# Five attention units by hand before block 0, weight decoding in quarters, and block 0 alone for sixteen slots

## The chip, the cores and the metric

The kernel runs on one core of one Trainium2 chip. The metric is the device time of one execution in microseconds; lower is better.

## The reference

The input is a linear attention with a decaying state over 4 batches, 8 heads, 768 steps and head dimension 48. Its output, 3072 tokens of 384 values, goes through two feed-forward layers with 2048 hidden values each. Everything is float32.

```python
for t in range(S):                                   # S = 768
    cur = einsum('bhd,bhe->bhde', u * k[t], v[t])
    y[t] = einsum('bhd,bhde->bhe', r[t], state + cur)
    state = w[..., None] * state + einsum('bhd,bhe->bhde', k[t], v[t])
x = y as (3072, 384)
h = x @ w_in1;  x = max(0.01 * h, h) @ w_out1        # layer 0
h = x @ w_in2;  x = (h * cos(h)) @ w_out2            # layer 1
```

## The kernel before

**Attention** is cut into 24 units of 128 tokens, six for each batch, and each unit into two chunks of 64. Units 0 to 7 (`u < ONE`) are built by `early(u)`, which returns the steps of a unit by name: `X R Z` (VectorE: the keys, queries and a third tensor times powers of the decay), `PK` and `NK` (32 matmuls, then a ScalarE copy), `PA` and `PD` (32 matmuls of scores each), `M N` (two VectorE selects out of PSUM), `PU S1 PV S0` (the new state; a "lean" unit does the state's sums on VectorE, the others fold them into matmuls and copy on ScalarE). `piece_y1` makes the output of the unit, which GpSimd's DMA queue writes to `xt` in DRAM (line 493), reads back as `xl` (`load_xu`, line 563), and `split_xu` splits into a high and a low part (a ScalarE cast at line 567, a VectorE subtraction at 568). Units 8 to 23 run through `prep`, `piece_a` and `piece_y` with fewer steps.

**The feed-forward layers** run over 12 blocks of 512 tokens (6 in each layer) times 16 weight chunks. One such pair is a slot. `g1` has nine matmuls of 128x128 by 128x512 (line 580), `evac_a` and `evac_b` evacuate it (for layer 0: ScalarE line 589, VectorE 590, ScalarE 607, VectorE 608), and two slots later (`LAG`) `g2` has nine matmuls into three accumulators (lines 620 to 622). So 192 slots have 3456 large matmuls.

**Weights** come packed, 768 KB for a chunk (`load_w`, line 140), and `split_w` decodes one with three ScalarE instructions (lines 281, 285, 286) and five of VectorE (282, 283, 290, 291, 294).

**Order.** SyncE's DMA queue runs in program order. For ScalarE, VectorE and TensorE the list `first` writes the order by hand for units 0 to 3 with four whole decodes; all after it is ordered by a planner that simulates the timeline. Block 0 is alone for `LB` = 8 slots, and the rest of block 0 alternates with block 1. Units 5 to 7 lie in the first slots of block 0, each chunk is decoded just before its first slot, and weight chunks 13 to 15 are loaded after the output of unit 7, since their buffers are lent to attention (the three states `ss_`, the keys `nk_`, one output). Units from 8 on are put into the slots by `due`; block 2 needs units 8 to 11.

Of the kernel before, what the change touches and what calls it, by code (L numbers as in the profile page):

```python
# [21 lines left out]
HC = C // 2  # L22
# [14 lines left out]
LB = 8  # L37
GB = 2
LATE = 8
HOLD = 16  # L40
# [3 lines left out]
FIRST = 3  # L44
# [13 lines left out]
def moe_rwkv_kernel(ctx: ExitStack, tc, wT, uT, wq, uu, rs, ks, nat, wmoe, out):  # L58
# [36 lines left out]
    ss_ = [halves(lent(*i)) for i in ((15, 0), (15, 1), (14, 0))]  # L95
    nk_ = halves(lent(14, 1))
    nk_ = [nk_[:, i] for i in range(2)]
# [53 lines left out]
    for f in range(4):  # L151
        load_w(0, f)
# [28 lines left out]
    for i in range(4):  # L181
        nc.gpsimd.memset(vf_[i][64:128, 0], 0.0)
        nc.gpsimd.memset(vf_[i][0:64, 1], 0.0)
        if i < 3:
            nc.gpsimd.memset(ss_[i], 0.0)
    sm = ap_.tile([D, H, D], F32, name="sm")
    ub = ap_.tile([128, H, D], F32, name="ub")

    def decays():
        nc.vector.tensor_scalar(out=ws, in0=wt, scalar1=W_LO, scalar2=W_HI, op0=ALU.max, op1=ALU.min)  # L190
        for i in range(H):
# [7 lines left out]
        nc.gpsimd.tensor_tensor(out=wd, in0=wc, in1=wc, op=ALU.mult)  # L199
# [9 lines left out]
    def in_range():  # L209
        ge = const.tile([PACK, H], F32, name="ge")  # L210
        cnt = const.tile([PACK, 1], F32, name="cnt")
        flag = const.tile([1, 1], I32, name="flag")
        nc.vector.tensor_tensor(out=ge, in0=ws, in1=wt, op=ALU.is_equal)
        nc.vector.tensor_reduce(out=cnt, in_=ge, axis=AX.X, op=ALU.min)
        tot = psum.tile([1, 1], F32, tag="a1", name="tot")
        nc.tensor.matmul(out=tot, lhsT=cnt, rhs=ones, start=True, stop=True)
        nc.vector.tensor_scalar(out=flag, in0=tot, scalar1=PACK - 0.5, scalar2=None, op0=ALU.is_lt)
        return nc.values_load(flag[0:1, 0:1], min_val=0, max_val=1)
# [55 lines left out]
    def split_w(L, f):  # L274
# [11 lines left out]
        nc.scalar.copy(out=mid[:, :, :, 0], in_=part[:, :, :, 1])  # L286
# [10 lines left out]

# [4 lines left out]
    def early(u):  # L302
        x, r, z, ar, vs = kf_[ring(u)], rf_[ring(u)], zf_[u % 2], ar_[u % 2], v_of(u)
        n, st = nk_[u % 2], ss_[u % 3]
        s0, s1 = st[HALF[1], 0], st[HALF[0], 1]
        nxt = (ss_[(u + 1) % 3] if u + 1 < ONE else vs_[1 - u % 2])[HALF[1], 0]
        last = u % NCH == NCH - 1
        first, lean = u % NCH == 0, u >= UB
# [38 lines left out]
        def PU():  # L347
            o = bank_of("pu")
            fold = not first and not lean
            if fold:  # L350
                nc.tensor.matmul(out=o[HALF[1]], lhsT=ident[0:PACK, HALF[1]], rhs=st[0:PACK, 0], start=True, stop=False)
# [39 lines left out]
    E = {}  # L391
# [29 lines left out]
    def piece_a(u):  # L421
        if u < ONE:
            return step("PK NK PA PD PU S1 PV S0 M N", u)
# [52 lines left out]
    def piece_y1(u):  # L476
        ar = ar_[u % 2]
        vs, ss = (t.rearrange("t c h d -> t (c h d)") for t in (v_of(u), ss_[u % 3]))
        py = psum.tile([PACK, H, HC], F32, tag=f"{bank(u)}2", name="py")
        for g in range(H):  # L480
# [4 lines left out]
            for c in range(1 if u % NCH == 0 else 0, 2):  # L485
                nc.tensor.matmul(
                    out=py[HALF[c], g], lhsT=ss[0:PACK, cols(H * c + g, D)], rhs=rf_[ring(u)][:, g],
                    start=False, stop=True)
        yo = yo1 if u % 2 else ap_.tile([PACK, H, HC], F32, tag="yo", bufs=YOB, name="yo")
# [22 lines left out]
    def do_piece():  # L512
# [8 lines left out]
        else:  # L521
            piece_y(i)
            if i == ONE - 1:
                for f in range(13, NF):
                    load_w(0, f)
            if i + 2 >= 6:
                fetch(i + 2)
# [57 lines left out]
    def evac_a(slot):  # L585
        p = hp.pop(slot)
        ga = mp.tile([128, NB], F32, tag="ga", bufs=2, name="ga")
        if blocks[slot[0]][0] == 0:
            nc.scalar.activation(out=ga, in_=p, func=AF.Copy, scale=0.01)  # L589
            nc.vector.tensor_tensor(out=ga, in0=p, in1=ga, op=ALU.max)  # L590
        else:
            gt = mp.tile([128, NB], F32, tag="gt", bufs=2, name="gt")
            nc.scalar.activation(out=ga, in_=p, func=AF.Copy, scale=INV2PI, bias=0.25)  # L593
            nc.scalar.activation(out=gt, in_=ga, func=AF.Copy, bias=MAGIC)  # L594
            nc.vector.scalar_tensor_tensor(  # L595
                out=gt, in0=gt, scalar=MAGIC, in1=ga, op0=ALU.subtract, op1=ALU.subtract)
            nc.vector.tensor_scalar(  # L597
                out=gt, in0=gt, scalar1=0.5, scalar2=-0.5, op0=ALU.min, op1=ALU.max)
            nc.scalar.activation(out=gt, in_=gt, func=AF.Sin, scale=-TWOPI)  # L599
            nc.vector.tensor_tensor(out=ga, in0=p, in1=gt, op=ALU.mult)  # L600
        ev[slot] = ga
# [46 lines left out]
    for j in range(1, N1):  # L648
        a = 0 if j == 1 else at[0][1] + LAG + 1 if j == 2 else at[2][0] + PACE * (j - 3)
        b = a + PACE if j > 2 else at[j][0] - (2 if j == 1 else 4)  # L650
        n = ends[j] - ends[j - 1]
        for q in range(FIRST if j == 1 else 0, n):
            due.setdefault(a + (b - a) * q // n, []).append(q)

    def decode():
        split_w(0, ready[0])
# [6 lines left out]
    def decode2():  # L663
# [4 lines left out]
        split_w(1, ready2[0])  # L668
# [14 lines left out]
    with tc.manual_schedule(engines={mybir.EngineType.Activation, mybir.EngineType.DVE, mybir.EngineType.PE}):  # L683
        decays()
        for k, u in first:
            if k == "if":
                slow = in_range()
                step_by_step()
                rest_of_loads()
            elif k not in do:  # L690
                step(k, u)
            else:
                do[k](u)
                if k == "y":
                    load_xu(u)
    for f in range(10, 13):
        load_w(0, f)
    kn = ap_.tile([128, H, D], F32, name="kn")
    ps = psum.tile([128, H, D], F32, tag="a1", name="ps_t")
    for c, g, a, b in flip(pt[:, 1]):  # L700
        nc.tensor.matmul(out=ps[TOK[c], g], lhsT=a, rhs=b, start=True, stop=True)
    nc.scalar.copy(out=kn, in_=ps)
    npc[0] = ends[0]
    while npc[0] < ends[0] + FIRST:
        do_piece()
    split_xu(UB - 1)

    for si in range(len(slots) + LAG):
        if si < len(slots):
            slot = j, f = slots[si]  # L710
            while j == 0 and ready[0] < min(f + AHEAD, NF):
                decode()
            g1(slot)
            evac_a(slot)
        if 1 <= si <= len(slots):
            evac_b(slots[si - 1])
        if si < len(slots):
            for _ in due.get(si, ()):
                do_piece()
            if npc[0] >= len(pieces) and not rest:  # L720
# [55 lines left out]
```

## Time and profile before

| | |
|---|---|
| median of three runs | 965.49 us (964.47 to 969.25) |
| the profiled execution | 967.88 us |
| its span, from the first to the last instruction | 966.3 us |
| TensorE busy | 918.0 us, 95% of the span |
| VectorE busy | 634.6 us, 66% |
| ScalarE busy | 543.9 us, 56% |

The 1.58 us between the profiled execution and its span lie outside the instructions. Busy TensorE is not TensorE at its peak: its matmuls overlap, and small ones count as busy too.

### The profile page before, as it was taken

The page shows a single profiled execution, that of the slowest core. Times are in us where ns is not written, and L with a number is a line of the kernel's source. Part 1 is how long each engine was busy: PE and PEld are TensorE (multiplying, and loading weights), DVE is VectorE, ACT ScalarE, POOL GpSimd, SP SyncE. Part 2 cuts the span into 40 slices and gives each one's busy share as a digit, 9 for nine tenths or more (in the row PEclk, how much of TensorE's full clock was granted, in tenths as well). Part 3 has the DMA queues.
Part 4 walks back from the last instruction along what each step waited for, and adds up shares of the span by engine and source line. Part 5 has one row for each costly group of instructions (what it writes and reads, how often), then busy time and mean ns, then how long its engine had stood idle before and what let it go on. Part 6 is the DMA issues. An engine that isn't in the chain of part 4 may idle for free.

```text
span 966.3 us, 16453 instructions
## 1 busy us (share of the span) xinstructions
PE 918.0 (95%) x6536; PEld 759.3 (79%) x6536; DVE 634.6 (66%) x1042; ACT 543.9 (56%) x1043; POOL 53.2 (6%) x93
## 2 busy tenths in 40 slices
PE   5747998999999999999999999999999999999997
PEld 4746786888777888888788888888888888888886
DVE  6379938338875667574776986666656655665654
ACT  2456536434664555453746786665665655665654
POOL 3111110000100000000000000000000000000000
PEclk9867999999999999999999999999999999999999
DMA  7931143004431242231514520010100100100000
GB/s 241 303 114 55 43 139 78 1 22 127 148 117 51 84 122 65 61 115 48 199 33 164 164 98 34 21 46 1 33 34 1 51 16 1 65 1 1 34 1 33
DMA packets 31552, 71.55 MB, mean 74 GB/s; under 512 B 4464, under 2 KB 7664, under 8 KB 31472
## 3 DMA queue, kind: packets, MB, share of 16 engines
q1 hardware_dynamic: 21824, 47.66, 15.8%
q0 software_dynamic: 4896, 14.16, 4.8%
q10 hardware_dynamic: 4752, 8.65, 2.4%
q8 instruction: 51, 0.84, 0.4%
q14 instruction: 29, 0.24, 0.1%
HBM read 56.30 MB, written 14.16 MB: 73 GB/s over the span
## 4 chain that ended last, share of the span: by engine, by line
PE 79%; DVE 7%; DMA 6%; ACT 2%; issue 2%; SPq 0%; POOL 0%; DVEq 0%; ACTq 0%; POOLq 0%
PE ph L580 37%; PE po L620 13%; PE po L621 12%; PE po L622 12%; DMA raw<-in_wmoe 3%; PE py L465 1%; PE pa L429 1%; DMA kst<-in_ks 1%; PE pu L436 1%; DMA xt<-lent 1%; DVE w L290 1%; DVE gl L608 1%; DVE ar L405 1%; DVE ar L442 1%; DMA ar<-in_rs 1%
## 5 line engine op out<-in xcount | busy, mean ns | idle before, releaser
L580 PE MATMUL ph<-xh,w 128*128 128x512 f32 x1152 | 301.6, 390 | 0.0
L580 PEld LDWEIGHTS ph<-xh,w 128*128 128x128 f32 x1152 | 217.2, 189 | 45.6
L620 PE MATMUL po<-gh,w 128*128 128x512 f32 x576 | 227.6, 395 | 4.3 <-ACT gh L607 4.1
L621 PE MATMUL po<-gh,w 128*128 128x512 f32 x576 | 224.6, 390 | 0.0
L622 PE MATMUL po<-gl,w 128*128 128x512 f32 x576 | 208.1, 390 | 0.0
L608 DVE TENSOR_TENSOR gl<-ga,gh 128x512 fp32r<-128x512 f32 x192 | 132.3, 689 | 115.1 <-ACT gh L607 102.7
L607 ACT CAST gh<-ga 128x512 fp32r<-128x512 f32 x192 | 118.8, 619 | 134.2 <-PE po L621 91.6
L580 PE MATMUL ph<-xl,w 128*128 128x512 f32 x576 | 167.5, 394 | 3.1 <-DVE ga L590 3.1
L620 PEld LDWEIGHTS po<-gh,w 128*128 128x128 f32 x576 | 108.1, 188 | 28.9 <-ACT gh L607 5.7
L580 PEld LDWEIGHTS ph<-xl,w 128*128 128x128 f32 x576 | 108.1, 189 | 26.5 <-DVE ga L590 4.0
L622 PEld LDWEIGHTS po<-gl,w 128*128 128x128 f32 x576 | 107.9, 188 | 22.6
L621 PEld LDWEIGHTS po<-gh,w 128*128 128x128 f32 x576 | 108.2, 188 | 21.5
L590 DVE TENSOR_TENSOR ga<-ph,ga 128x512 f32<-128x512 f32 x96 | 66.0, 689 | 47.8 <-ACT ga L589 47.3
L589 ACT ACTIVATE ga<-ph 128x512 f32<-128x512 f32 x96 | 56.9, 594 | 64.6 <-PE ph L580 63.0
L595 DVE SCALAR_TENSOR_TENSOR gt<-gt,ga 128x512 f32<-128x512 f32 x96 | 65.9, 690 | 38.7 <-ACT gt L594 38.3
L600 DVE TENSOR_TENSOR ga<-ph,gt 128x512 f32<-128x512 f32 x96 | 65.8, 688 | 34.3 <-ACT gt L599 33.6
L599 ACT ACTIVATE gt<-gt 128x512 f32<-128x512 f32 x96 | 59.9, 627 | 49.2 <-DVE gt L597 48.9
L593 ACT ACTIVATE ga<-ph 128x512 f32<-128x512 f32 x96 | 57.4, 597 | 42.5 <-PE ph L580 29.2
L441 ACT ACTIVATE ar<-ident,bon 64x64 f32<-64x64 f32 x256 | 64.5, 333 | 17.0 <-DVE bon L408 16.7
L594 ACT ACTIVATE gt<-ga 128x512 f32<-128x512 f32 x96 | 60.3, 631 | 2.1 <-ACT ga L593 0.4
L597 DVE TENSOR_SCALAR gt<-gt 128x512 f32<-128x512 f32 x96 | 40.4, 424 | 1.9
L281 ACT ACTIVATE ds<-raw 128x768 f32<-128x768 f32 x32 | 29.1, 913 | 17.0 <-DMA raw<-in_wmoe 12.6
(134 smaller groups left out, 787.4 us busy)
## 6 DMA issues: line engine op xcount, KB each, us to landing
raw<-in_wmoe SPq DMA_DIRECT2D x32, 768.0 KB, 7.2
natt<-in_nat SPq DMA_DIRECT2D x16, 384.0 KB, 3.7
kst<-in_ks SPq DMA_DIRECT2D x22, 224.0 KB, 3.2
x2t<-ob ACTq DMA_DIRECT2D x18, 256.0 KB, 2.0
xl<-x2t POOLq DMA_DIRECT2D x6, 768.0 KB, 4.8
vs<-in_nat SPq DMA_DIRECT2D x44, 96.0 KB, 3.7
xt<-yo POOLq DMA_DIRECT2D x40, 96.0 KB, 3.3
out<-ob ACTq DMA_DIRECT2D x15, 256.0 KB, 2.0
```

The source lines that it names most:

```text
L441: nc.scalar.activation(out=ar[q, c, g], in_=ident2[q], func=AF.Copy, scale=bon[q, g:g + 1])
L580: nc.tensor.matmul(out=p, lhsT=w_[:, 0, k * 128:(k + 1) * 128], rhs=x_[:, k], start=(m == 0), stop=(m == 3 * KT - 1))
L590: nc.vector.tensor_tensor(out=ga, in0=p, in1=ga, op=ALU.max)
L594: nc.scalar.activation(out=gt, in_=ga, func=AF.Copy, bias=MAGIC)
L595: nc.vector.scalar_tensor_tensor(out=gt, in0=gt, scalar=MAGIC, in1=ga, op0=ALU.subtract, op1=ALU.subtract)
L599: nc.scalar.activation(out=gt, in_=gt, func=AF.Sin, scale=-TWOPI)
L600: nc.vector.tensor_tensor(out=ga, in0=p, in1=gt, op=ALU.mult)
L607: nc.scalar.copy(out=gh, in_=ga)
L608: nc.vector.tensor_tensor(out=gl, in0=ga, in1=gh.bitcast(F32), op=ALU.subtract)
L620: nc.tensor.matmul(out=o, lhsT=w_l[:, 1, sl], rhs=gh, start=(f == 0), stop=False)
L621: nc.tensor.matmul(out=o, lhsT=w_h[:, 1, sl], rhs=gh, start=False, stop=False)
L622: nc.tensor.matmul(out=o, lhsT=w_h[:, 1, sl], rhs=gl, start=False, stop=(f == NF - 1))
```

## The change

Five units (`SOLO`) instead of four are ordered by hand ahead of block 0. Their states live in two pairs of tiles that share the buffers of `gt` and `ob`, which the layers use later, and `nk_` in `kn` and `ub`, whose own contents are made after unit 7 (`late_tables`). The lent weight buffers 14 and 15 are thereby free, weight chunks 8 to 15 are loaded after unit 4, and loads of units 8 and 9 are held until the first prep piece. `split_w` becomes a generator of four parts, and a `quarter` of it stands between the steps. The order by hand now reaches through the first 16 slots (`HAND`), which are all of block 0's; units 5 to 7 are spread over slots 0 to 12, with four quarters of decoding in each slot until the weights are done. The second half of a unit's step, `PU S1 PV S0`, waits in the list `after` until the slot's `g2`. The range test (`flag`) is computed at the start instead of after unit 0's scores, `wd` moves from GpSimd to VectorE, and six matmuls of zeros (`stir`) run at the start.

```diff
-LB = 8
+LB = 16
-HOLD = 16
+HOLD = 99
-FIRST = 3
+SOLO = 5
+HAND = 16
...
-    ss_ = [halves(lent(*i)) for i in ((15, 0), (15, 1), (14, 0))]
-    nk_ = halves(lent(14, 1))
+    ss_ = [[mp.tile([128, NB], F32, tag=n, bufs=2, name=n)[:, 0:DM].rearrange("p (h d) -> p h d", h=H)
+            for n in ("gt", "ob")] for i in range(2)]
+    nk_ = [kn, ub]
...
+    def stir(n):
+        o = psum.tile([128, DM], F32, tag="h", bufs=2, name="stir")
+        for i in range(n):
+            nc.tensor.matmul(out=o, lhsT=still[:, 0:128], rhs=still, start=i == 0, stop=i == n - 1)
...
     def decays():
...
+        nc.vector.tensor_tensor(out=ge, in0=ws, in1=wt, op=ALU.is_equal)
+        nc.vector.tensor_reduce(out=cnt, in_=ge, axis=AX.X, op=ALU.min)
+        stir(3)
+        nc.tensor.matmul(out=tot, lhsT=cnt, rhs=ones, start=True, stop=True)
+        stir(3)
...
+        nc.vector.tensor_scalar(out=flag, in0=tot, scalar1=PACK - 0.5, scalar2=None, op0=ALU.is_lt)
...
-        nc.gpsimd.tensor_tensor(out=wd, in0=wc, in1=wc, op=ALU.mult)
+        nc.vector.tensor_tensor(out=wd, in0=wc, in1=wc, op=ALU.mult)
...
     def split_w(L, f):
...
+        nc.scalar.copy(out=mid[:, :, :, 0], in_=part[:, :, :, 1])
+        yield
         nc.scalar.activation(out=s, in_=top.bitcast(F32), func=AF.Sign)
+        yield
...
         nc.scalar.activation(out=a, in_=a, func=AF.Relu, scale=8.0, bias=rebias)
-        nc.scalar.copy(out=mid[:, :, :, 0], in_=part[:, :, :, 1])
+        yield
...
-        first, lean = u % NCH == 0, u >= UB
+        first, lean = u % NCH == 0, u >= SOLO
...
-            return step("PK NK PA PD PU S1 PV S0 M N", u)
+            return step("PK NK PA PD M N", u) or after.append(("PU S1 PV S0", u))
...
+    first = [("R Z", 0), ("X R Z", 1), ("if", 0), ("PK NK PA PD M N", 0), ("d", 0)]
+    for u in range(SOLO - 1):
+        first += [("PK NK", u + 1), ("d", 0), ("PU S1", u), ("d", 0), ("PA", u + 1), ("PV S0", u),
+                  ("PD", u + 1)]
+        first += [("X R Z", u + 2)] if u + 2 < SOLO else [("x", 0)]
+        first += [("d", 0), ("d", 0), ("y", u)]
+        first += {0: [("l", 4), ("w", 5)], 1: [("l", 5), ("w", 6), ("w", 7)]}.get(u, [])
+        first += [("M N", u + 1)]
+    u = SOLO - 1
+    first += [("PU S1 PV S0", u), ("x", 1), ("x", 2), ("y", u), ("l", 6)] + [("w", f) for f in range(8, NF)]
+    first += 3 * [("d", 0)] + [("x", 3), ("X R Z", SOLO), ("d", 0), ("d", 0)]
...
     for si in range(len(slots) + LAG):
+        if si == HAND:
+            hand.close()
         if si < len(slots):
             slot = j, f = slots[si]
-            while j == 0 and ready[0] < min(f + AHEAD, NF):
-                decode()
             g1(slot)
+        if si < HAND:
+            e0, e1 = evac_0(slot), evac_2(slot)
+            next(e0)
+            quarter()
+            next(e0)
+            next(e1)
+            quarter()
+            next(e1)
+        elif si < len(slots):
             evac_a(slot)
...
             for _ in due.get(si, ()):
                 do_piece()
+            if si < HAND:
+                quarter()
+                quarter()
+            if npc[0] >= ends[1] and not late_split:
+                late_split.append(1)
+                split_xu(2 * UB - 1)
...
             g2(slots[si - LAG])
+            while after:
+                step(*after.pop(0))
```

## Rows read from the trace of the kernel before

**Rows 1.** Stretches: PE, PEld, DVE, ACT, POOL busy us; granted clock, DMA share, GB/s.
```profile
0.00:20.00 20.00, 8.57 (x139) 8.13 (x140) 12.84 (x30) 4.86 (x13) 8.80 (x27) 1.00 0.83 261
20.00:40.00 20.00, 19.66 (x457) 17.78 (x456) 8.79 (x14) 9.90 (x15) 2.42 (x3) 1.00 0.82 275
40.00:80.00 40.00, 22.71 (x399) 20.84 (x399) 25.86 (x41) 19.67 (x28) 7.01 (x9) 0.66 0.46 141
80.00:120.00 40.00, 33.24 (x457) 28.13 (x457) 38.86 (x63) 23.60 (x34) 4.76 (x6) 0.91 0.18 48
120.00:160.00 40.00, 35.11 (x341) 29.08 (x338) 24.95 (x41) 17.17 (x26) 4.06 (x6) 0.96 0.44 131
160.00:966.30 806.30, 798.75 (x4755) 655.35 (x4753) 523.35 (x857) 468.75 (x929) 26.20 (x42) 1.00 0.19 60
```

**Rows 2.** TensorE's instruction groups up to 160 us: count, busy us and mean ns.
```profile
L580 PE MATMUL ph<-xh,w 128*128 128x512 f32 x72 | 19.3, 405 | 0.0
...
L620 PE MATMUL po<-gh,w 128*128 128x512 f32 x28 | 11.4, 407 | 2.6 <-ACT gh L607 2.6
```

**Rows 3.** The chain of waits: start us, us it took, what.
```profile
34.92 11.46 DMA kst<-in_ks
...
63.61 0.57 ACT lent L490
...
75.65 0.52 ACT xh L567
...
117.53 2.04 PE ph L580 x9
...
121.53 1.06 PE pk L331 x32
...
125.90 0.43 PE po L620
...
130.21 0.26 PE py L482 x3
132.25 0.60 ACT lent L490
...
136.84 7.63 DMA raw<-in_wmoe
```

**Rows 4.** VectorE in order of time: start, us, instruction, idle before and releaser.
```profile
10.17 0.16 DVE L204 TENSOR_TENSOR uw<-ut,ws 112x8 f32<-112x8 f32 x1
...
17.85 0.73 DVE L344 COPY_PREDICATED ar<-mask,pa 128x512 f32<-128x512 int32 x1 [1.35 <-DVEq L221]
...
27.40 0.96 DVE L290 TENSOR_TENSOR w<-dt,ds 128x768 fp32r<-128x768 f32 x1 [5.24 <-ACT dm L286]
...
46.41 0.69 DVE L319 TENSOR_TENSOR kst<-kst,pt 112x512 f32<-112x512 f32 x1 [12.21 <-DMA kst<-in_ks]
...
92.31 0.55 DVE L282 TENSOR_SCALAR dt<-raw 128x768 int32<-128x768 int32 x1
...
97.28 0.69 DVE L319 TENSOR_TENSOR kst<-kst,pt 112x512 f32<-112x512 f32 x1
```

**Rows 5.** TensorE in order of time, in units 0 to 2.
```profile
12.48 1.91 PE L340 MATMUL pa<-ar,kst 48*64 48x64 f32 x30
...
28.18 0.85 PE L351 MATMUL pu<-lent,ident 112*48 112x384 f32 x2
...
35.81 0.25 PE L331 MATMUL pk<-ident,lent 48*64 48x48 f32 x1
```

**Rows 6.** ScalarE in order of time: the casts of two reloaded units.
```profile
100.10 0.51 ACT L567 CAST xh<-xl 128x384 fp32r<-128x384 f32 x1 [1.67 <-DMA xl<-xt]
...
129.01 0.52 ACT L567 CAST xh<-xl 128x384 fp32r<-128x384 f32 x1 [5.89 <-DMA xl<-xt]
```

**Rows 7.** GpSimd's DMA issues for the outputs of the same two units.
```profile
93.00 1.67 POOL L493 DMA_DIRECT2D xt<-yo  x2 [19.58 <-ACT yo L490]
...
122.44 1.27 POOL L493 DMA_DIRECT2D xt<-yo  x2 [9.54 <-ACT yo L490]
```

More of the change, by code (lines that the diff above doesn't have):

```diff
@@ L150, in moe_rwkv_kernel @@
         load(u)
-    for f in range(4):
+    for f in range(5):
         load_w(0, f)
@@ L207, in decays @@
                 out=dg[HALF[0], i], in_=ident[HALF[0], HALF[0]], func=AF.Copy, scale=wd[HALF[0], i:i + 1])
[L209 to L218, printed above, removed]
+        return flag
     def step_by_step():
@@ L350, in PU @@
             if fold:
-                nc.tensor.matmul(out=o[HALF[1]], lhsT=ident[0:PACK, HALF[1]], rhs=st[0:PACK, 0], start=True, stop=False)
+                nc.tensor.matmul(out=o[HALF[1]], lhsT=ident[0:PACK, HALF[1]], rhs=st[0][0:PACK], start=True, stop=False)
             for g in range(H):
@@ L486, in piece_y1 @@
                 nc.tensor.matmul(
-                    out=py[HALF[c], g], lhsT=ss[0:PACK, cols(H * c + g, D)], rhs=rf_[ring(u)][:, g],
+                    out=py[HALF[c], g], lhsT=ss[c][0:PACK, g], rhs=rf_[ring(u)][:, g],
                     start=False, stop=True)
-        yo = yo1 if u % 2 else ap_.tile([PACK, H, HC], F32, tag="yo", bufs=YOB, name="yo")
+        yo = yo1 if u % 2 and u < UB else ap_.tile([PACK, H, HC], F32, tag="yo", bufs=YOB, name="yo")
         nc.scalar.copy(out=yo, in_=py)
@@ L523, in do_piece @@
             if i == ONE - 1:
[L524 to L527, printed above, removed]
+                late_tables()
+            fetch(i + 2)
             if i < 2 * UB:
@@ L585, in evac_a, with evac_0, evac_1, evac_2 @@
     def evac_a(slot):
+        for _ in evac_0(slot) if blocks[slot[0]][0] == 0 else evac_1(slot):
+            pass
+    def evac_0(slot):
         p = hp.pop(slot)
[L587 to L601, printed above, removed]
+        ga = ev[slot] = mp.tile([128, NB], F32, tag="ga", bufs=2, name="ga")
+        nc.scalar.activation(out=ga, in_=p, func=AF.Copy, scale=0.01)
+        yield
+        nc.vector.tensor_tensor(out=ga, in0=p, in1=ga, op=ALU.max)
+        yield
+    def evac_1(slot):
+        p = hp.pop(slot)
+        ga = ev[slot] = mp.tile([128, NB], F32, tag="ga", bufs=2, name="ga")
+        gt = mp.tile([128, NB], F32, tag="gt", bufs=2, name="gt")
+        nc.scalar.activation(out=ga, in_=p, func=AF.Copy, scale=INV2PI, bias=0.25)
+        nc.scalar.activation(out=gt, in_=ga, func=AF.Copy, bias=MAGIC)
+        nc.vector.scalar_tensor_tensor(
+            out=gt, in0=gt, scalar=MAGIC, in1=ga, op0=ALU.subtract, op1=ALU.subtract)
+        nc.vector.tensor_scalar(
+            out=gt, in0=gt, scalar1=0.5, scalar2=-0.5, op0=ALU.min, op1=ALU.max)
+        nc.scalar.activation(out=gt, in_=gt, func=AF.Sin, scale=-TWOPI)
+        nc.vector.tensor_tensor(out=ga, in0=p, in1=gt, op=ALU.mult)
+        yield
     def evac_b(slot):
+        for _ in evac_2(slot):
+            pass
+    def evac_2(slot):
         ga = ev.pop(slot)
@@ L650, in moe_rwkv_kernel @@
         b = a + PACE if j > 2 else at[j][0] - (2 if j == 1 else 4)
-        n = ends[j] - ends[j - 1]
-        for q in range(FIRST if j == 1 else 0, n):
+        n = ends[j] - (ends[j - 1] if j > 1 else pieces.index(("p", SOLO)) + 2)
+        for q in range(n):
             due.setdefault(a + (b - a) * q // n, []).append(q)
     def decode():
-        split_w(0, ready[0])
+        for _ in split_w(0, ready[0]):
+            pass
         ready[0] += 1
@@ L667, in decode2, with late_tables @@
                 load_w(1, i)
-        split_w(1, ready2[0])
+        for _ in split_w(1, ready2[0]):
+            pass
         ready2[0] += 1
-    def rest_of_loads():
-        for f in range(4, 8):
-            load_w(0, f)
+    def late_tables():
         nc.sync.dma_start(out=ub, in_=uu)
-    do = {"w": lambda f: load_w(0, f), "y": piece_y, "l": load, "d": lambda f: decode(), "x": split_xu}
-    first = [("R Z PK NK PA PD", 0), ("X R Z", 1), ("if", 0), ("M N", 0),
[4 rows of a table removed]
[L683 to L706, printed above, removed]
+        ps = psum.tile([128, H, D], F32, tag="a1", name="ps_t")
+        for c, g, a, b in flip(pt[:, 1]):
+            nc.tensor.matmul(out=ps[TOK[c], g], lhsT=a, rhs=b, start=True, stop=True)
@@ new lines, in late_tables, with quarter @@
+        nc.scalar.copy(out=kn, in_=ps)
+    part = []
+    def quarter():
+        if ready[0] == NF:
+            return
+        if not part:
+            part.append(split_w(0, ready[0]))
+        if next(part[0], part) is part:
+            ready[0] += 1
+            part.clear()
+    do = {"w": lambda f: load_w(0, f), "y": piece_y, "l": load, "d": lambda f: quarter(), "x": split_xu}
+    first = [("R Z", 0), ("X R Z", 1), ("if", 0), ("PK NK PA PD M N", 0), ("d", 0)]
[6 more added lines that the diff above has]
+        first += [("M N", u + 1)]
@@ new lines, in moe_rwkv_kernel @@
+    u = SOLO - 1
+    first += [("PU S1 PV S0", u), ("x", 1), ("x", 2), ("y", u), ("l", 6)] + [("w", f) for f in range(8, NF)]
+    first += 3 * [("d", 0)] + [("x", 3), ("X R Z", SOLO), ("d", 0), ("d", 0)]
+    hand = ExitStack()
+    hand.enter_context(tc.manual_schedule(
+        engines={mybir.EngineType.Activation, mybir.EngineType.DVE, mybir.EngineType.PE}))
+    flag = decays()
+    for k, u in first:
+        if k == "if":
+            slow = nc.values_load(flag[0:1, 0:1], min_val=0, max_val=1)
+            step_by_step()
+        elif k not in do:
+            step(k, u)
+        else:
+            do[k](u)
+            if k == "y":
+                load_xu(u)
@@ L714, in moe_rwkv_kernel @@
             evac_a(slot)
-        if 1 <= si <= len(slots):
+        if HAND < si <= len(slots):
             evac_b(slots[si - 1])
```

35 lines of the change are left out of this document (21 added, 14 removed), and 4 rows, old and new, of the table first.

## The prediction

> **What bounds the kernel now.** First the table of stages. From 160 us on TensorE is busy 798.75 of 806.3 us at the full clock, so 7.6 us is all that is idle there, and a change can only remove work or move the moment at which this stage begins [rows 1]. Ahead of 160 us TensorE sits idle 40.7 us of 160, in 40 to 120 us partly at the lower granted clock, and VectorE is busy 38.9 of 40 us from 80 to 120 us [rows 1]. Second, the list of groups up to 160 us shows how little of the large work is then done: 72 of the six `xh` matmuls that each slot has, so 12 `g1`, and 28 of the three of line 620, so 9.3 `g2` [rows 2]. Third, the chain of waits prices that work when nothing disturbs it: nine large matmuls in 2.04 us, 0.2267 us each, 4.08 us a slot [rows 3]. The 3456 − 108 − 84 = 3264 matmuls left at 160 us are 739.9 us; with the idle 7.6 us the 16 late attention units are the remaining 806.3 − 739.9 − 7.6 = 58.8 us, 3.7 us each. Done by then are 192 × 0.2267 = 43.5 us of large matmuls and units 0 to 7. A lean early unit costs TensorE 4.4 us for its first five groups and 2.0 us for its output [rows 3], 6.4 us; eight are about 51 us. So 160 us hold some 95 us of TensorE work, and 65 us are the most that any order of the first stage could win.
>
> The same views say where they go: 12.2 us in which VectorE waits for the keys of unit 4, which SyncE's queue had put behind weight chunks; 5.2 us in which it waits for ScalarE in a whole decode that was emitted at one place [rows 4]; 7.6 us for weight chunks that are loaded after unit 7 [rows 3]; and TensorE between 80 and 120 us starved by VectorE.
>
> **The change, part by part.** All of it lies ahead of block 1, so I compute when slot 0 begins (T0), when slot 16 begins (T16), and add what is left.
>
> *Start.* The range test needs a VectorE compare and reduce before the scans, `flag` waits for a matmul behind three of `stir`, and `wd` comes to VectorE: about 1 us of small instructions, 0.7 us of waiting, an estimate. The decay work now ends at 10.3 us [rows 4], so unit 0's second half of keys is ready at about 11.9 us. In return the branch at 16.5 us is no longer preceded by a wait for the scores, but its own 1.35 us stays [rows 4]. `stir` runs while TensorE has nothing else. It may raise the clock earlier: 30 score matmuls at 12.48 us take 1.91 us, 64 ns each, where 32 matmuls of that size take 1.06 us later on [rows 5, 3]; by that pace this is the lower of the two levels, though the granted clock reads 1.00 there [rows 1]. If it doesn't help, some 10 us of TensorE work run at half pace, 5 us lost; without any stir that is what was paid before. I take the clock as full after unit 0.
>
> *Units by hand.* In an undisturbed stretch at full clock one unit of the folded kind, from its `PU` at 28.18 us to the next `PK` at 35.81 us, takes 7.6 us, and a `PK` 1.1 us more [rows 5, 3]: 8.7 us of TensorE. VectorE's share is smaller. One decode with three further instructions of about 0.6 us takes 97.28 − 92.31 = 5.0 us [rows 4], so a decode is 3.1 us, `X R Z` 1.9 us and `M N` 1.4 us: 6.4 us. In the new list each part that waits for ScalarE has `X R Z` between it and the part that uses it, so the 5.2 us go, and the 12.2 us go because weights 5 to 7 are issued one or two at a time behind the keys. ScalarE has less still: it was busy 23.6 us of the 40 in which VectorE was full [rows 1]. So the pace is TensorE's 8.7 us. With `PK PA PD` of unit 0 from 11.9 us to about 15 us, four rounds (the first without its fold, 0.7 us less) end at 49 us, and with them the matmuls of unit 3's output.
>
> *The step to slot 0.* Slot 0 needs unit 3 written and read back. That took 12.0 us from the output copy to the cast [rows 3] with weight loads on the queues, and 6.6 us after the issue, so 7.4 us with a copy of 0.57 us ahead, without them [rows 6, 7]. The rest of unit 4 (`PU S1 PV S0`, output: about 4.5 us), two splits and three quarters lie beside this wait. ScalarE and VectorE stand at `x 3`; behind it are only `X R Z` of unit 5 and the decode that slot 2 needs first. With 7.4 to 12 us and 1 us of splitting T0 is 57.5 to 62 us. I take 59; 5 us for a cold clock bring 65.
>
> *Sixteen slots.* When slot 16 begins, 16 `g1` and 14 `g2` are issued: 270 matmuls, 61.2 us. Units 5 to 7 add 19.2 us, the 32 matmuls of `late_tables` 1.1 us: 81.5 us on TensorE. VectorE in the first 10.5 slots, while weights are decoded, has 3.1 + 1.2 us a slot and 4.3 us for each of three units: 58 us; TensorE has in the same slots 42.8 − 4.1 + 19.2 = 58 us. Equal loads in queues that keep program order cost something: 0 to 0.5 us a slot, 0 to 8 us; I take 5, near the middle, since `g1` may run one slot ahead (two buffers). The weights are in time: chunks 8 to 15 are issued at some 54 us and the decode reaches chunk 8 at slot 2.5. The split of unit 7 stands behind its own output on ScalarE in slot 12, 7.4 us or more; TensorE has 1.1 us of tables and five groups of 2.04 us to do first, 11.3 us, so nothing is lost unless the round trip reaches its 12 us. T16 = 59 + 81.5 + 5 = 145.5 us.
>
> *The rest.* 3456 − 270 = 3186 matmuls, 722.2 us, the late units' 58.8 us and the old idle 7.6 us: 788.6 us. Units 8 to 11 get ten slots instead of three; the loads of units 8 and 9 stand on SyncE right behind the table load that waits for unit 7, ahead of their use. At best this saves half of the idle 7.6 us.
>
> Sum: 145.5 + 788.6 = 934.1 us of span, against 966.3. The profiled execution lies 1.6 us above its span and 2.4 us above the median, so the median becomes **933 us**.
>
> **Rivals.** (1) *The order by hand serialises the slots; slower.* If `max` of a slot stands behind the decode and the piece of the one before, and these behind ScalarE, a slot costs `g1` 2.04, two VectorE evacuations of 0.6 as in that 5.0 us stretch [rows 4], two on ScalarE taken as long, a decode's second part of 2.2 and 1 us of piece: 7.6 us, with hand-offs 8. Then T16 = 59 + 128 and the median is 974 us. It decides from (966.3 − 788.6 − 59) / 16 = 7.4 us a slot. For it: VectorE's load. Against: the buffers, and the long stretch from 80 to 120 us in which VectorE never stood still. Chance 0.07. (2) *A load still comes late*, unit 6's behind the output of unit 4, or chunk 8 behind it: the price of the old waits, 7.6 to 12.2 us [rows 3, 4], 941 to 945 us. Against: each now has over 10 us of lead. Chance 0.1. (3) *GpSimd's output chain is slowed by a busy VectorE.* The two rows stand for an issue with VectorE full (1.67 us, the cast 7.1 us after it) and with VectorE idle (1.27 and 6.6 us) [rows 7, 6]: 0.5 us, and if all of the 12.0 us were due to this, 4.6 us at T0 and some 1 us at unit 7: 939 us. The Trainium skill (SBUF — State Buffer, "SBUF: two separate sides") says that descriptors of DMAs issued by GpSimd can't be written while VectorE runs an operation in a mode with two ports, which would speak against a change that packs VectorE; the trace agrees in sign, with 0.4 us an issue. Chance 0.08. (4) *Nothing is gained*: the order is only as good as the two engines' balance and slots take 7.0 to 7.5 us. 960 to 968 us, chance 0.05.
>
> **The numbers.** The forecast, with its bounds, has 0.70: T0 57 to 65, friction 0 to 8 us, and 0 to 4 us won from late idle give 922 to 944 us by itself. Rivals 2 and 3 lie at its upper side, so the range that leaves out 2 in 10 is 921 to 951 us. Half a per cent, 4.8 us, is about what a measurement of this kernel tells from no change. Faster: 0.70 + 0.10 + 0.08 = 0.88; same 0.05; slower 0.07.
>
> **What would show it.** The first `ph` matmul at about 59 us, where before the cast that it needs starts at 75.65 us [rows 3]; the 16th evacuation by line 590's successor at about 145 us; no VectorE wait of 12 us for keys, and none of TensorE's for a weight decode; 8 to 9 us between the units' selects. The forecast is wrong if slots 0 to 10 are further apart than 6.5 us, if ScalarE's wait for the split of unit 3 or 7 reaches 12 us, or if TensorE's idle time after 160 us grows.

## The result and the profile after

The changed kernel takes 950.66 us (median of four runs, 948.72 to 954.78) against 966.09 us (four runs, 964.47 to 969.25): a ratio of 0.984, interval 0.980 to 0.988, so faster by 15.4 us. The forecast had 933 us, with a range of 921 to 951 us: the result lies just inside the range, but the gain forecast is twice the one measured. The profiled execution took 954.78 us, the slowest of the four, its span 953.2 us. TensorE is busy 917.5 us as before (918.0), VectorE 636.9 us (634.6); nearly all that changed is TensorE's idle time, 966.3 − 918.0 = 48.3 us before and 953.2 − 917.5 = 35.7 us after.

The stretches of the profile after, with the columns of [rows 1]:

```profile
0.00:20.00 20.00, 14.73 (x222) 10.46 (x222) 15.76 (x35) 7.74 (x17) 8.43 (x27) 1.00 0.83 266
20.00:40.00 20.00, 20.00 (x476) 18.28 (x475) 15.74 (x24) 11.12 (x17) 3.87 (x5) 0.91 0.76 247
40.00:80.00 40.00, 26.09 (x487) 22.32 (x483) 21.56 (x35) 17.83 (x27) 6.82 (x10) 0.83 0.68 233
80.00:120.00 40.00, 34.05 (x310) 28.06 (x309) 34.93 (x53) 24.60 (x35) 2.15 (x3) 0.91 0.08 22
120.00:160.00 40.00, 38.08 (x395) 31.32 (x393) 32.40 (x53) 24.23 (x57) 4.04 (x6) 1.00 0.27 75
160.00:953.20 793.20, 784.59 (x4692) 644.56 (x4692) 516.48 (x845) 458.97 (x894) 26.14 (x42) 1.00 0.19 61
```

TensorE does not stand still at all from 20 to 40 us, but from 40 to 120 us it still loses 20 of 80 us (24 before). Its list of waits up to 180 us begins with these three (waiting line, what it waited for: us in total, times, longest):

```profile
PE ph L591 <- DVE xl L579: 12.9, 1, 12.9
PE py L499 <- DVE ob L381: 5.1, 1, 5.1
PE ph L591 <- DVE ga L605: 3.8, 1, 3.8
```

None of the three old waits is among them: keys, a weight decode, late weights. In their place stand the first `ph` for the split of unit 3, an output for a state `ob`, and one slot's `ph` for an evacuation. The first, in ScalarE's order of time (start, us, instruction, idle before and releaser):

```profile
49.92 0.59 ACT L503 COPY lent<-py 112x512 f32<-112x512 f32 x1 [1.07 <-issue]
...
66.87 0.51 ACT L578 CAST xh<-xl 128x384 fp32r<-128x384 f32 x1 [9.42 <-DMA xl<-xt]
```

and in GpSimd's, which issues the output writes (line 506) and the readbacks (line 574):

```profile
44.07 0.75 POOL L574 DMA_DIRECT2D xl<-xt  x1 [6.00 <-DMA xt<-lent]
47.49 1.27 POOL L506 DMA_DIRECT2D xt<-yo  x2 [2.68 <-ACT gt L394]
51.18 0.76 POOL L574 DMA_DIRECT2D xl<-xt  x1 [2.42 <-DMA xt<-yo]
55.11 1.27 POOL L506 DMA_DIRECT2D xt<-lent  x2 [3.17 <-ACT xh L578]
59.71 0.75 POOL L574 DMA_DIRECT2D xl<-xt  x1 [3.33 <-DMA xt<-lent]
67.41 1.27 POOL L506 DMA_DIRECT2D xt<-yo  x2 [6.94 <-ACT xh L578]
```

Unit 3's output is copied at 49.92 us, 0.9 us from the forecast's 49. Its write starts 5.2 us after that, the readback 4.6 us later, and the cast 7.2 us after this: 17 us where the forecast had 7.4 to 12. Note what comes ahead of each write: at 55.11 us the readback that started at 51.18 has just landed (ScalarE cast it at 54.57 us), and at 67.41 us again the cast of the unit before. The releaser's name, a ScalarE cast, is inferred; that it is the readback itself had to be tested. The kernel before shows the same wait once, which the forecast didn't use. Unit 1 in ScalarE's order, then in GpSimd's:

```profile
35.92 0.59 ACT L490 COPY lent<-py 112x512 f32<-112x512 f32 x1 [0.32 <-PE py L486]
...
36.35 0.76 POOL L563 DMA_DIRECT2D xl<-xt  x1 [6.52 <-DMA xt<-yo]
45.53 1.29 POOL L493 DMA_DIRECT2D xt<-lent  x2 [8.42 <-ACT xh L567]
```

Its output is copied at 35.92 us and written at 45.53, 9.6 us later, behind the readback of unit 0 that started at 36.35.

Three stretches from slot 0 to slot 16, columns as above:

```profile
68.00:72.90 4.90, 4.88 (x34) 3.56 (x35) 2.77 (x6) 1.75 (x4) 0.67 (x2) 0.57 1.03 398
72.90:134.79 61.89, 55.94 (x594) 46.66 (x591) 56.31 (x86) 40.67 (x57) 4.93 (x7) 0.94 0.16 49
134.79:169.00 34.21, 29.53 (x226) 23.87 (x225) 21.68 (x36) 16.50 (x48) 2.02 (x3) 0.90 0.27 78
```

Slot 0 begins at 68.0 us (forecast 59), slot 16 at about 169 (forecast 145.5): 101 us for work that was put at 81.5 us plus 5. By these rows TensorE is idle 101.0 − 90.35 = 10.65 us. Below the full clock it works in slot 0 (first row) and in two stretches behind pauses:

```profile
90.12:97.00 6.88, 6.88 (x68) 6.08 (x69) 4.13 (x6) 1.12 (x2) 0.00 (x0) 0.57 0.21 64
162.76:169.00 6.24, 6.24 (x17) 4.95 (x18) 2.68 (x4) 2.33 (x4) 0.00 (x0) 0.60 0.00 1
```

The missing clock costs 4.90 × 0.43 + 6.88 × 0.43 + 6.24 × 0.40 = 7.6 us of work. After slot 16 remain 784.2 us (forecast 788.6). So the profiled span is the forecast's 934.1 + 9.0 + 14.5 − 4.4 = 953.2 us: all of the miss lies ahead of slot 0 and in the 16 slots.

Inside the slots, VectorE in order of time, slot 2:

```profile
84.77 0.55 DVE L296 TENSOR_SCALAR dt<-raw 128x768 int32<-128x768 int32 x1
85.24 0.59 DVE L297 TENSOR_SCALAR dm<-raw 128x768 uint16<-128x768 uint16 x1
85.73 0.67 DVE L605 TENSOR_TENSOR ga<-ph,ga 128x512 f32<-128x512 f32 x1
86.33 0.96 DVE L304 TENSOR_TENSOR w<-dt,ds 128x768 fp32r<-128x768 f32 x1
87.32 0.56 DVE L305 TENSOR_SCALAR dt<-w 128x768 int32<-128x768 int32 x1
87.92 0.96 DVE L308 SCALAR_TENSOR_TENSOR w<-dm,dt 128x768 fp32r<-128x768 int32 x1
88.79 0.68 DVE L633 TENSOR_TENSOR gl<-ga,gh 128x512 fp32r<-128x512 f32 x1
89.51 0.56 DVE L381 TENSOR_TENSOR ob<-pu,gt 48x384 f32<-48x384 f32 x1
```

No idle time stands in brackets: VectorE runs without a pause, 89.51 − 84.77 = 4.74 us for a decode and two evacuations (the forecast took 3.1 + 1.2 = 4.3). The state `ob` of unit 5, for which TensorE's in-order queue stands still for 5.1 us until 90.12 us, comes last in that line, since its step sits in the list `after`, behind the slot's `g2`. The third wait is in ScalarE's order around slot 12:

```profile
148.88 4.03 ACT L454 ACTIVATE ar<-ident,bon 64x64 f32<-64x64 f32 x16 [2.14 <-DVE bon L421]
...
153.46 0.58 ACT L503 COPY yo<-py 112x512 f32<-112x512 f32 x1
...
154.78 4.03 ACT L454 ACTIVATE ar<-ident,bon 64x64 f32<-64x64 f32 x16
160.97 0.51 ACT L578 CAST xh<-xl 128x384 fp32r<-128x384 f32 x1 [2.16 <-DMA xl<-xt]
161.39 0.59 ACT L603 ACTIVATE ga<-ph 128x512 f32<-128x512 f32 x1
```

The cast of unit 7 stands ahead of the next slot's evacuation and waits for its readback, 7.5 us after the output copy; preparations of later units (line 454, twice 4.03 us) have come into the same queue. The first of them stands ahead of unit 7's output copy: the matmuls of that output start last at 147.23 us, the copy at 153.46. The second lies beside the round trip; the cast waits 2.16 us more for the data. Evacuations of line 605 start at 148.77 and then only at 162.01 us.

### The profile page after: what moved, and what is told of

Same layout as the page of the kernel before. It is cut to its first block, busy times and chain, and to the rows that moved or that the text cites. A ratio compares the mean times of both kernels' runs of the same rounds, so it can differ in the third digit from the quotient of the medians.

```text
span 953.2 us, 16526 instructions
## 1 busy us (share of the span) xinstructions
PE 917.5 (96%) x6566; PEld 755.0 (79%) x6566; DVE 636.9 (67%) x1041; ACT 544.5 (57%) x1045; POOL 51.5 (5%) x93
## 4 chain that ended last, share of the span: by engine, by line
PE 80%; DMA 2%; ACT 2%; DVE 2%; issue 1%; SPq 0%; POOL 0%; ACTq 0%; POOLq 0%; DVEq 0%
PE ph L591 37%; PE po L645 13%; PE po L646 12%; PE po L647 12%; PE py L478 2%; PE pa L442 2%; PE pu L449 1%; DMA raw<-in_wmoe 1%; DMA natt<-in_nat 1%; ACT ar L454 0%; DVE gl L633 0%; DMA xl<-xt 0%; DVE w L304 0%; ACT gh L631 0%; ACT dt L299 0%
## 5 line engine op out<-in xcount | busy, mean ns | idle before, releaser
L647 PE MATMUL po<-gl,w 128*128 128x512 f32 x576 | 211.0, 390 | 0.0
L591 PE MATMUL ph<-xl,w 128*128 128x512 f32 x576 | 166.9, 393 | 16.8 <-DVE xl L579 12.9
L292 ACT COPY dm<-raw 128x768 uint16<-128x768 uint16 x32 | 34.5, 1079 | 14.0 <-DMA raw<-in_wmoe 12.4
```

Source lines behind the costliest of these rows:

```text
L591: nc.tensor.matmul(out=p, lhsT=w_[:, 0, k * 128:(k + 1) * 128], rhs=x_[:, k], start=(m == 0), stop=(m == 3 * KT - 1))
L647: nc.tensor.matmul(out=o, lhsT=w_h[:, 1, sl], rhs=gl, start=False, stop=(f == NF - 1))
```

## The experiments

Theory: the forecast's work is right, and the gain is lost to (A) the write of unit 3, which waits for the readback of unit 2, (B) the eight weight loads beside that readback, (C) the split of unit 7 ahead of an evacuation, (D) the state of unit 5 behind three slots' decoding. Rivals: TensorE's clock after its pauses, and VectorE as the bound of the decoding slots. Ratios are to the kernel before on the same chip; the change stands at 0.9842.

**e1, weight chunks 8 to 15 held until unit 3 is cast.**

```diff
+          "g": lambda u: nc.sync.dma_start(out=mark, in_=xs[0][0][0:1, 0, NB - 1:NB].bitcast(F32))}
...
-    first += [("PU S1 PV S0", u), ("x", 1), ("x", 2), ("y", u), ("l", 6)] + [("w", f) for f in range(8, NF)]
-    first += 3 * [("d", 0)] + [("x", 3), ("X R Z", SOLO), ("d", 0), ("d", 0)]
+    first += [("PU S1 PV S0", u), ("x", 1), ("x", 2), ("y", u), ("l", 6)]
+    first += 3 * [("d", 0)] + [("x", 3), ("g", 3)] + [("w", f) for f in range(8, NF)] + [("X R Z", SOLO), ("d", 0), ("d", 0)]
```

> Weight chunks 8 to 15 are issued only after the cast of unit 3 (a 4-byte DMA that reads the cast's result stands ahead of them on SyncE's queue). Theory A: slot 0 is held by the round of output writes and readbacks on GpSimd's queue, and the weights slow only its last leg (readback of unit 3 issued at 59.7 us, cast at 66.9 us): that leg falls from 7.1 to about 3.5 us, the first ph matmul from 68.0 to about 64.5 us, the time from 950.7 to 946-948 us. Rival B: the weights are the whole delay against the forecast of 59 us: first ph at 59-60 us, 942 us or less. Rival C: what was mis-sized is the cost of the sixteen slots, and an earlier slot 0 is given back there: first ph earlier, time within 2 us of 950.7.

951.65 us, ratio 0.984 (0.980 to 0.987): no gain. The last leg did shrink, from 7.2 us to 67.57 − 64.65 = 2.9 us, but in this profile unit 3's output was copied at 54.56 us instead of 49.92, and the cast came at 67.57 us. That copy comes before the edit acts, so the later slot 0 isn't its doing (the spread of this copy is taken up below). B lengthens a leg; alone it is worth nothing that the times show.

**e2, the readback at a fixed address.** It leaves out the choice of the step-by-step result, which the register in the address makes for inputs out of range.

```diff
-        src = xt[bass.ds(slow, 1), :, u * C:(u + 1) * C].rearrange("o (k p) t -> p (o k) t", p=128)
+        src = xt[0:1, :, u * C:(u + 1) * C].rearrange("o (k p) t -> p (o k) t", p=128)
```

> The readback of units 0 to 7 reads the first half of xt at a fixed address instead of at one held in a register, so it leaves out the choice of the step-by-step result for blocks 0 and 1. Theory A1: each output write waits for the readback before it because that read, whose address is not known, counts as touching every column: the write of unit 3 is issued right after its copy (about 50.8 instead of 55.1 us), its cast comes at 60-62.5 us instead of 66.9, first ph at 62-64 us, time 944-947 us. Rival A2: the wait is the queue's own order (a DMA on GpSimd's queue starts when the one before has landed): the issue times stay, 950-951 us.

947.15 us, ratio 0.980 (0.978 to 0.983): 3.5 us less than the change in the medians, though their intervals overlap. GpSimd in order of time:

```profile
47.57 0.76 POOL L574 DMA_DIRECT2D xl<-xt  x1 [2.33 <-DMA xt<-yo]
53.62 1.27 POOL L506 DMA_DIRECT2D xt<-lent  x2 [5.30 <-ACT lent L503]
57.86 0.75 POOL L574 DMA_DIRECT2D xl<-xt  x1 [2.97 <-DMA xt<-lent]
58.93 1.41 POOL L506 DMA_DIRECT2D xt<-yo  x2 [0.31 <-ACT yo L503]
```

Now each write follows its own copy: unit 3's, copied at 52.74 us, is written at 53.62 and cast at 61.46 us, 8.7 us in all where the change has 17. Unit 4's write no longer waits for unit 3's readback either. TensorE's wait falls from 12.9 to 5.4 us. A is shown by the trace: the wait goes when the register leaves the address. That a read whose address is open counts as touching columns it doesn't read, so that the program keeps the next write behind it, is the likely reason; it is argued, not shown.

**e3, the split of unit 7 at slot 15.**

```diff
-            if npc[0] >= ends[1] and not late_split:
+            if npc[0] >= ends[1] and si >= HAND - 1 and not late_split:
```

> The split of unit 7 is moved from slot 12 to slot 15 in the order by hand; nothing else changes. Theory H: in slot 12 ScalarE stands at this cast for the round trip of the output (issue 154.3, cast 161.0), the evacuation of slot 13 comes behind it and TensorE idles 3.8 us and falls to the lower clock: those go, time 944-947 us. Rival: TensorE only uses that time for pieces of units 8 and 9 that are due anyway, and the wait moves to another evacuation: 949-951 us.

947.23 us, ratio 0.980 (0.977 to 0.983): 3.4 us less than the change, again with intervals that overlap. The stretch after slot 11:

```profile
140.00:180.00 40.00, 40.00 (x313) 32.89 (x312) 24.93 (x42) 20.56 (x55) 2.03 (x3) 1.00 0.30 89
```

TensorE is busy all of 40 us at the full clock (36.19 us at 0.91 in the change), and no wait for that evacuation is left. C is shown by the trace.

**e4, the state steps in `after` run in slots 0 and 1 too.**

```diff
-            while after:
-                step(*after.pop(0))
+        while after:
+            step(*after.pop(0))
+        if si >= LAG:
```

> The second half of unit 5's step (PU S1) is emitted in slot 0, after its scores, instead of after the first g2 in slot 2. Theory H: TensorE's 5.1 us wait in slot 3 for the state that VectorE writes at 89.5 us, behind three slots of decoding, goes: time 944-946 us if no other wait takes its place. Rival D: VectorE is the bound of slots 0 to 10, and the 5.1 us only show it; the wait moves to an evacuation of the same slots: 949-951 us.

950.95 us, ratio 0.984 (0.980 to 0.988). The wait of 5.1 us is gone and slot 4 is evacuated at 95.77 us instead of 100.62, but the median is the change's (950.66). The two profiles show less of a loss: slot 18 is evacuated at 176.90 us instead of 180.35, so of the 4.9 us won at slot 4 some 1.4 are given back, part of them at the split of unit 7, whose wait is 4.4 us now instead of 3.8. The change's profiled run was its slowest (954.78 us, here 951.16), and each ratio is uncertain by 0.004, 3.9 us. D is a real wait; what its removal is worth in time this run can't tell.

**e5, without the matmuls of zeros.** 

```diff
-        stir(3)
         tot = psum.tile([1, 1], F32, tag="a1", name="tot")
         nc.tensor.matmul(out=tot, lhsT=cnt, rhs=ones, start=True, stop=True)
-        stir(3)
```

> The six matmuls of zeros at the start are left out. If they bring units 0 and 1 to the higher clock (key matmuls of 220 ns instead of 263 ns before the change), these units fall back to the slow pace, the copy of unit 0's output comes some 3-5 us later than 24.9 us, and through the round of writes and readbacks slot 0 with it: 952-956 us. If TensorE's clock is not what the round waits for, the time stays at 950-951 us.

951.79 us, ratio 0.985 (0.981 to 0.988). Unit 0's output is copied at 24.39 us, in the change at 24.87. Zeros at the start are worth nothing that can be measured.

**e6, the four edits of e1 to e4 together.** Like e2, it and e8, e9, e10 and e12 leave out the choice of the step-by-step result.

> All four edits at once: weights 8 to 15 behind the cast of unit 3, readback at a fixed address, split of unit 7 in slot 15, state of unit 5 in slot 0. If the losses are separate places of one chain, they add: the readback 3.5 us, its last leg up to 3 more, the split 3.4, the state 0 to 4: 938-943 us. If VectorE bounds the sixteen slots whatever stands ahead, most is given back there: 945-947 us, no better than the best single edit.

938.41 us, ratio 0.971 (0.968 to 0.974): 12.2 us below the change in the medians, 0.0132 in the ratio, with intervals far apart, and faster than both kernels. One by one the edits sum to 0.0085; the uncertainty of the four ratios, up to 0.004 each, covers the difference. TensorE's waits up to 180 us keep one long entry, 5.4 us before slot 0; the next is 2.1 us.

**e7, 14 matmuls of zeros just ahead of slot 0 of the change.**

```diff
+    stir(14)
     npc[0] = pieces.index(("p", SOLO)) + 2
```

> As changed, with 14 more matmuls of zeros (about 9 us) on TensorE between unit 4's output and slot 0, where it sits idle for 12.9 us. They delay nothing. Clock theory: TensorE is at the lower level from 59 to 72 us because it was idle, slot 0 and unit 5's matmuls run at half pace, and that is 2.5-3 us lost on the way: 947-948 us. If VectorE bounds slots 0 to 3, the faster slot 0 waits for it: 950-951 us.

958.28 us, ratio 0.993 (0.991 to 0.995), 7.6 us worse than the change. Slot 0 begins at 68.5 us, its granted clock from 68 to 72 us is 0.69 (0.50 in the change), and slot 18 is evacuated at 180.62 us (180.35 in the change): the zeros neither win nor lose there. Both expectations failed. The two profiles differ by 2.1 us, all of it after 180 us (775.3 against 773.2 us); why, and where the rest of the 7.6 us is, isn't explained.

**e8, the same line on top of e6.**

> The four edits together with the 14 matmuls of zeros ahead of slot 0, which now may reach past the arrival of unit 3's cast by some us. If idle time ahead of slot 0 is short with the four edits, the zeros only delay it: 1-4 us more than the four alone. If the clock is still lost in that gap, 1-3 us less.

940.58 us, ratio 0.975 (0.972 to 0.979), not better than e6. Here the granted clock is 1.00 from 56 to 76 us, and the first `ph` starts at 63.18 us. From it to the 16th evacuation at 151.14 us it takes 88.0 us; in e9, whose clock is 0.50 from 62 to 66 us, 151.55 − 62.00 = 89.6 us. So a full clock from slot 0 on is worth some 1.6 us in the slots, and the zeros take more than that: the first `ph` comes 5.2 us after unit 3's cast, in e9 2.4.

**e9, e6 with five zeros instead of three in the second `stir`.**

```diff
-        stir(3)
+        stir(5)
```

> The four edits of e6_four, and eight matmuls of zeros at the start instead of six, so that TensorE is idle for less time between them and unit 0's scores. In the profile of e6_four the first units ran at the lower clock after that gap (granted 0.58 from 12 to 20 us), in other runs they didn't. If that gap is what costs e6_four its cast of unit 3 at 63.9 us instead of some 59, the copy of unit 3's output comes near 50 us and the time falls by 3-5 us against e6_four: 934-936 us. If the clock falls anyhow: within 1 us of e6_four.

937.57 us, ratio 0.973 (0.971 to 0.976), as e6. Its granted clock is 0.50 from 12 to 20 us all the same. In its profile slot 0 begins at 62.0 us, the 16th evacuation at 151.55 us, and slot 13's `g2`, behind which slot 16 begins in the order by hand, ends at 151.7 us.

**e10, only A and B of e6; e11, only C and D.**

> Only the two edits ahead of slot 0: readback at a fixed address and weights 8 to 15 behind unit 3's cast. Theory: what the forecast lacked at slot 0, 9 us, is the round of writes and readbacks and its last leg; without both the cast of unit 3 comes at 58-63 us, depending on the clock of the first units, and the time is 943-946 us. Rival: the weights are then late for the slots (they start to load at some 60 us), and the time stays at the 947 us of the fixed address alone.

> Only the two edits in the slots: split of unit 7 in slot 15 and state of unit 5 in slot 0. If the 5 us that the state wins are given back in the wait for unit 7, as the run with that edit alone suggests, they now count, and the time is 942-945 us. If VectorE takes them back: 947 us, as with the split alone.

947.21 us, ratio 0.981 (0.979 to 0.984), and 946.35 us, ratio 0.979 (0.975 to 0.982). A and B together give what A gives alone, as the rival had it. C and D together give 0.0057, which lies between theory and rival. The halves add up to 0.0086 of e6's 0.0132; with ratios that are each uncertain by 0.002 to 0.004 this neither shows nor excludes that the edits help each other, and what D is worth beside C (0.980 alone, 0.979 with D) isn't resolved either.

**e12, e6 with one VectorE decode instruction (about 0.5 us) issued twice for chunks 6 to 15.** 

```diff
+        if L == 0 and f >= 6:
+            nc.vector.tensor_scalar(
+                out=mid[:, :, :, 1], in0=part[:, :, :, 2], scalar1=0x1FF, scalar2=None, op0=ALU.bitwise_and)
```

> The four edits of e6_four, and one of VectorE's five decode instructions (0.5 us) issued twice for chunks 6 to 15: 5 us more of VectorE work in slots 0 to 10. If VectorE bounds these slots, 4-5 us more than e6_four: 942-944 us. If TensorE does, with VectorE only near it, 0-2 us: 938-940 us.

944.82 us, ratio 0.981 (0.978 to 0.984): 6.4 us above e6, 7.2 above e9, more than the 4 to 5 expected. From slot 2 to slot 15 the evacuations take 158.78 − 81.08 = 77.7 us, in e9 151.55 − 80.49 = 71.1 us: 6.6 us more for 5 us of VectorE work. The stretches between the evacuations of slots 1 and 10, in e9 and then here (columns of [rows 1]):

```profile
74.04:123.66 49.62, 46.94 (x484) 39.18 (x483) 48.82 (x77) 36.21 (x51) 4.04 (x6) 0.97 0.21 66
...
73.99:129.56 55.57, 50.14 (x491) 40.92 (x489) 54.34 (x86) 36.35 (x50) 4.04 (x6) 0.94 0.18 58
```

VectorE is busy 48.82 of 49.62 us and 54.34 of 55.57 us: it is all but full in both; its work grows by 5.5 us and the stretch by 6.0. TensorE waits for two ScalarE copies, in e9 2.7 and 0.9 us:

```profile
PE pu L370 <- ACT kn L351: 4.5, 1, 4.5
PE pu L370 <- ACT ub L351: 2.4, 1, 2.4
```

With the four edits VectorE, not TensorE, sets the pace while weights are decoded.

## Why the forecast was right in sign and off in size

**Start and units by hand: right.** The second half of unit 0's keys is ready at 11.6 us (forecast 11.9), unit 3's output copied at 49.9 (49). The second is in part luck: in the thirteen profiles of the change and its variants this copy comes at 49.2 to 55.3 us. The spread goes with a pause of TensorE in unit 2's output, for which the profile names no cause, and the clock behind it: in e8 (49.2) there is no pause and the granted clock is 1.00 from 40 to 52 us, in e1 (54.6) the pause is 2.3 us and the clock 0.77 and 0.81 from 44 to 52 us, in e6 (55.3) 0.7 and 1.8 us, 0.50 and 0.65. In e11 (54.4) unit 0 is already late, its copy at 28.28 us. That the clock is full after unit 0 is not a property of the change: it was so in this profile, not in most others (last section), and e5 shows that the zeros which should have brought it are worth nothing in time.

**The step to slot 0: the first failed step.** "7.4 to 12 us" was read from two round trips in the kernel before, in which the writes didn't wait for a readback [rows 3, 6, 7]. In the new order the next unit's output is ready before the last readback has landed, and each write waits for that. T0 was 68 us instead of 59; e2 takes the wait away, and the step is 8.7 us long, inside the forecast's bounds. So the price was right for one unit, and the missed term is the queue of the units, put at nothing: 5.2 us ahead of unit 3's write alone. The kernel before showed it at unit 1, 9.6 us. The weight loads' share of the leg (7.2 against 2.9 us in e1, 3.6 us in e2) disappears with it: the readback then starts before the loads fill the queues.

**Sixteen slots: the second, and the larger.** "I take 5" for friction measured 10.65 us of idle time and 7.6 us of clock; the 1.3 us left over are work above the 81.5 us. Two entries are single waits. The state of unit 5 (5.1 us) is named nowhere in the forecast, which costed `after` at nothing. The split of unit 7 was said to lose nothing, since TensorE had 11.3 us of work beside a round trip of 7.4 to 12 us. TensorE had that work, and the round trip took 7.5 us from the copy; but the copy came 6.2 us after the output's matmuls, behind preparations for later units that the planner had put into ScalarE's queue, and the split holds back an evacuation whose `ph` buffer TensorE needs. The clock's share follows the waits: e3 and e4 show the full clock, or nearly, in the stretch whose wait they take away (140 to 180 us in e3; 88 to 96 us at 1.00 in e4, 0.66 and 0.50 in the change).

**"Equal loads of 58 us": mis-sized.** A slot's decode and evacuations take VectorE 4.74 us in slot 2, and in e9 two evacuations with no attention between them lie 85.11 − 80.49 = 4.62 us apart: not 4.3, so over 10.5 slots 3.4 to 4.6 us more than TensorE's share. Most of that is the decode. From slot 2's lines it takes 3.42 us instead of 3.1: line 304 gives way to the next after 0.99 us and line 305 after 0.60, where each next one reads what the one before wrote. In the kernel before other work stood between, and the same two instructions (290, 291) gave way after 0.87 us (to 97.28 us) and 0.46 us:

```profile
93.28 0.55 DVE L291 TENSOR_SCALAR dt<-w 128x768 int32<-128x768 int32 x1
93.74 0.68 DVE L608 TENSOR_TENSOR gl<-ga,gh 128x512 fp32r<-128x512 f32 x1
...
96.41 0.95 DVE L290 TENSOR_TENSOR w<-dt,ds 128x768 fp32r<-128x768 f32 x1
```

That the dependence is the reason is argued from these rows; no run reorders them. e12 says that VectorE is the bound there. Between slot 0 and slot 16 e9's profile still has 89.7 us (62.0 to 151.7) against the forecast's 86.5. That these 3.2 us are the larger decode is argued, not shown: TensorE also has 4.0 us at a clock of 0.50 in slot 0.

**The rest: a little better than forecast**, 784.2 against 788.6 us; from 180 us on TensorE is idle 773.2 − 767.34 = 5.9 us.

**The rivals.** (1) Serial slots at 7.4 us didn't occur: evacuations 0 to 10 take 134.79 − 72.90 = 61.9 us, 6.2 a slot with the wait of 5.1 us in it. (2) No load that the rival names came late; up to 180 us VectorE waits 2.6 us in all for inputs of units after 7. (3) On the way to slot 0 it didn't occur: unit 3's write takes 1.27 us to issue, and so does unit 7's (154.33 us), with VectorE busy throughout. But a slowed issue exists. GpSimd in order of time, and last an instruction of VectorE during the first row:

```profile
25.77 1.83 POOL L506 DMA_DIRECT2D xt<-yo  x2 [15.77 <-ACT yo L503]
...
127.25 1.27 POOL L506 DMA_DIRECT2D xt<-yo  x2 [24.76 <-ACT yo L503]
...
26.14 0.60 DVE L297 TENSOR_SCALAR dm<-raw 128x768 uint16<-128x768 uint16 x1
```

Of the eight such issues for units 0 to 7 the two long ones, 1.83 us and 1.40 us (98.22 us), lie beside the one-input instructions of the decode (lines 296, 297), as the 1.67 us of before does (283, 291). Beside two-input instructions alone (308, 633 at 127.25 us) it is 1.27 us, the same as with VectorE nearly idle [rows 7]; one issue beside lines 296 and 297 (55.11 us) also took 1.27. The rule of the Trainium skill (SBUF — State Buffer, "SBUF: two separate sides") that the forecast weighed fits these rows; which instructions run in the mode that it names, no row says. It costs 0.1 to 0.6 us an issue here, not the 4.6 us of the rival. (4) "Nothing is gained" is ruled out by the interval.

Of its own signs the forecast failed by the first two: the first `ph` came at 68.0 us and the 16th evacuation at 167.69. TensorE's idle time after 160 us grew too, from 7.6 to 8.6 us. The slots were 6.2 us apart, under its limit of 6.5. Two of its sums are slightly off: 59 and 5 make 64, not 65, and its bounds add up to 942 at the top, not 944; neither bears on the miss.

With the four edits the forecast's 933 us (0.966) is approached to 938 (0.971). What is left fits the decode and the spread of the first units; no run takes either away.

## What to carry to other kernels

When an order by hand packs work closer, ask of every DMA what the next one on its buffer waits for: a round trip measured in a loose schedule doesn't hold the waits that a tight one adds, and here the wait went when the read's address no longer came from a register. In an in-order queue, look at what stands ahead of a small instruction that another engine needs; one state sum of 0.56 us behind three slots of decoding cost 5.1 us. And where several waits lie in a row, removing one may show nothing in the median (e4), so look in the trace where the time it frees goes before dropping the edit. Instructions that read each other's results back to back took up to 0.14 us longer each than with other work between them; a price from an interleaved stretch doesn't hold for them.

## What the hardware showed that was not expected

From 55 to 169 us of the change TensorE's granted clock falls in or behind each of the three long pauses (12.9, 5.1 and 3.8 us) and stays at the lower level into the work that follows; in the stretches between (72.9 to 84.9, 97 to 158.9 us) it is 1.00. After the pause of 3.8 us, in which TensorE waits for slot 13's evacuation, in order of time:

```profile
162.76 1.65 PE L591 MATMUL ph<-xl,w 128*128 128x512 f32 x3 [3.81 <-DVE ga L605]
164.20 2.76 PE L591 MATMUL ph<-xh,w 128*128 128x512 f32 x6
...
169.31 0.85 PE L591 MATMUL ph<-xl,w 128*128 128x512 f32 x3
170.00 1.52 PE L591 MATMUL ph<-xh,w 128*128 128x512 f32 x6
```

The same nine matmuls take 4.2 us at a granted clock of 0.53 (164 to 168 us) and 2.2 us at 1.00 (168 to 172 us): the levels of 1.2 and 2.4 GHz. So a wait on the path costs more than its length: behind this one the missing clock is 6.24 × 0.40 = 2.5 us, on top of the 3.8.

At the start the same program falls on either side. After the zeros TensorE pauses once more for the keys, and of twelve profiles with zeros the clock from 12 to 20 us read 1.00 in two (the change and e4) and 0.50 to 0.62 in ten. The matmuls' pace bears this out: 32 scores of unit 0 take 1.15 us in those two and 1.97 us in e1. The reading alone doesn't suffice, for in e5, without zeros, it is 1.00 while the same scores take 1.94 us. What decides it isn't known, and the time doesn't follow it: e1 with 0.50 has the change's time, e9 with 0.50 is among the fastest.
